# Values' two parts in one 128-column stationary block, and global queries' softmax transposed in float32 without a copy

## The chip, the cores and the metric

The kernel runs on one core of one Trainium2 chip. The time is device microseconds (us) of one execution on that core; a run's figure is a median over repeated executions. The profile is that of one execution, and its span is the time from the first to the last recorded instruction.

## The reference, cut to what matters

Attention with local and global tokens is followed by a two-layer network with a gated activation. All arrays are float32.

```python
B, H, Sl, D = 8, 8, 512, 64;  Sg = 32           # batch, heads, local and global tokens, head size
k_all = concat([k_g, k_l]); v_all = concat([v_g, v_l])
out_g = softmax(q_g @ k_all.T / 8) @ v_all      # each global query sees all 544 keys
s_ll  = where(|i - j| <= 32, q_l @ k_l.T / 8, -1e9)
out_l = softmax([q_l @ k_g.T / 8, s_ll]) @ concat([v_g, v_l])
x = concat([out_g, out_l]).transpose(0, 2, 1, 3).reshape(4352, 512)
h = x @ w_in                                    # 512 -> 2048
out = (h * sigmoid(h)) @ w_out                  # 2048 -> 512
```

## The kernel before, in words

**Tiles and blocks.** The 4352 rows of x are 34 tiles of 128 rows. They form 12 blocks (`SIZES`: two, ten times three, two tiles). For a block `n`, `first_layer(n, f)` makes one of 16 slices `f` of h (L563, 12 matmuls), ScalarE and VectorE apply the activation (L569 to L576), and `second_layer(n, f)` adds the slice into the block's output banks (L588 to L590), one slice later. Block 0 does this in float32 (L557, L586); from block 1 on every operand is split into a high and a low part in the faster float32r format (hi = rounded copy, lo = rest), and a product is three matmuls: hi times hi, hi times lo, lo times hi.

**Attention steps.** Attention for the local rows is cut into 128 steps `k`. A step takes one batch entry `b`, one chunk `c` of 128 rows (four of them, `NC`), and one of four head pairs `pr` (`NPR`); the two heads of a pair are `u` = 0 and 1. A step's parts are:

- `st_load`, `st_vload`: DMAs of queries, keys and values from HBM, issued on SyncE's queue (SP).
- `st_split`, `st_vsplit` (from step `KF` = 24 on, which is the 25th step): float32 to float32r parts. For the values these are `vhi` (ScalarE, L322) and `vlo` (VectorE, L323).
- `st_scores`: scores `s` (L345), band mask and minimum (L349), exponential (L353), normalising (L355 to L358), and from step 24 on a DMA copy to `rr`, whose tile is declared float32r (L365).
- `st_turn`: four TensorE transposes (L380; L378 in float32 for steps below 24) into a PSUM bank `t`; ScalarE and VectorE write the parts `pt_hi` and `pt_lo` of the transposed probabilities (L389, L390). Columns 128 to 159 of `pt` hold the global queries' transposed probabilities for the same keys; GpSimd (POOL) copies them from `pgt` (L400, L401).
- `st_out`: the product with the values into PSUM bank `o`. A local step has two key tiles `a`. With `u` and `a` and the three products this is twelve matmuls a step, each with 64 stationary columns (L423). 160 columns are streamed where the global queries take part, else 128 (`a` = 1 in the chunks `c` = 0 to 2). Then, for each `u`, ScalarE takes `xh` (L434) and VectorE `xl` (L435) out of the bank, and VectorE adds the 32 global columns to `acc` (L440, L442).

**Global queries.** `g_load`, `g_split`, `g_scores` (L228 to L230) and `g_soft` make, for each batch entry, the softmax of the global queries in two tiles `pgs[hh]` of 128 x 544 float32. For `b` >= `GF` = 2, `g_move` copies such a tile by two DMAs into float32r tiles `r0` and `r1` (L258, L259; `r0` shares its buffers with the output tiles of L599). `g_turn` transposes them: four 128 x 128 transposes into a bank `o` (`gt`, L276) and one of 128 x 32 into a bank `s` (`gu`, L279), and ScalarE copies both to `pgt` (L277, L280). For `b` < 2 the transposes read the float32 tile itself.

**Banks.** While block 0 is prepared there are three banks for `s`, two for `t` and three for `o`. After that there is one of each, so that each new `o`, `gt` or second `gs` waits until the last content of bank `o` has been read, and a new `s` until `gu` has been copied.

**What sets the order.** Every part of a step has a due time in steps (`DUE`, `HEAD`, `TURN`, `MOVE`); `stream` is sorted by it. `fill` deals the stream out between the matmuls of the two layers. TensorE's instructions stay in the order in which they are written; those of the other engines, and the DMA issues on SP, are put in order at build time by a scheduler with its own time estimates. Each engine runs its queue strictly in order.

Of the kernel before, what the change touches and what calls it, by code (L numbers as in the profile page):

```python
# [9 lines left out]
F32 = mybir.dt.float32  # L10
# [41 lines left out]
MOVE, TURN = (-0.3, -0.8), (0.7, 1.7)  # L52
MOVE0, TURN0 = (0.1, 0.8), (1.5, 3.6)
# [5 lines left out]
def attention_moe_kernel(ctx: ExitStack, tc: tile.TileContext, qk0_in, qk_in, v_in, gqk, wts, out):  # L59
# [154 lines left out]
    def g_scores(b, p):  # L214
        did(("scores", b, p), *([("turn" if b <= GF else "move", b - 1, p // 2)] if b else []))
# [36 lines left out]
    def g_move(b, hh):  # L252
        did(("move", b, hh), ("soft", b, hh))
        if b < GF:
            return
        r0 = two.tile([P, 4 * P], F32R, tag="o", name=f"rg0_{b}_{hh}")
        r1 = two.tile([P, SG], F32R, tag="rg", name=f"rg1_{b}_{hh}")
        nc.sync.dma_start(out=r0.bitcast(F32), in_=pgs[hh][:, : 4 * P])  # L258
        nc.sync.dma_start(out=r1.bitcast(F32), in_=pgs[hh][:, 4 * P :])  # L259
        state["rg", hh] = r0, r1  # L260

    def g_turn(b, hh):
        whole = b < GF
        if whole:
            r0, r1, idt = pgs[hh], pgs[hh][:, 4 * P :], ident.bitcast(F32)
        else:
            (r0, r1), idt = state.pop(("rg", hh)), ident
        did(("turn", b, hh), ("turn", b, 0) if hh else ("last", b - 1))
        if hh == 0:
            state["pgt"] = work.tile([P, 5, H, SG], F32, tag="pgt", name=f"pgt{b}")  # L270
        pgt = state["pgt"]
        hs = slice(4 * hh, 4 * hh + 4)
        tb = attbank("o", f"gt{b}_{hh}")
        for i in range(4):
            sl = slice(i * P, (i + 1) * P)
            nc.tensor.transpose(tb[:, sl] if whole else tb[:, sl].bitcast(F32R), r0[:, sl], idt)  # L276
        nc.scalar.copy(out=pgt[:, 0:4, hs, :], in_=tb.rearrange("p (t h q) -> p t h q", t=4, h=4))  # L277
        tb = attbank("s", f"gu{b}_{hh}")
        nc.tensor.transpose(tb[:SG, :P] if whole else tb[:SG, :P].bitcast(F32R), r1, idt)  # L279
        nc.scalar.copy(out=pgt[:SG, 4, hs, :], in_=tb[:SG, :P].rearrange("p (h q) -> p h q", h=4))  # L280
# [35 lines left out]
    def st_vsplit(k, b, c, pr):  # L316
# [3 lines left out]
        vhi = two.tile([P, 2, 2, D], F32R, tag="vhi", name=f"vhi{k}")  # L320
        vlo = two.tile([P, 2, 2, D], F32R, tag="vlo", name=f"vlo{k}")
# [3 lines left out]
        tiles["v", k] = vhi, vlo  # L325
# [42 lines left out]
    def st_turn(k, b, c, pr):  # L368
# [12 lines left out]
        t4 = t.rearrange("p (u a q) -> p u a q", u=2, a=2)  # L381
        if whole:
            pt = tiles["pt", k] = pt_whole(k)
            if c == NC - 1:
                nc.gpsimd.memset(pt[:, :, 1, P:], 0.0)
            nc.scalar.copy(out=pt[:, :, :, :P], in_=t4)
        else:
            pt_hi, pt_lo = pt_tiles(k)
            nc.scalar.copy(out=pt_hi[:, :, :, :P], in_=t4)  # L389
            nc.vector.tensor_tensor(out=pt_lo[:, :, :, :P], in0=t4, in1=pt_hi[:, :, :, :P].bitcast(F32),  # L390
                                    op=ALU.subtract)
        did(("last", b) if (c, pr) == (NC - 1, NPR - 1) else k, ("turn", b, pr // 2))
        pgt = state["pgt"]
        for a in range(2 if c == NC - 1 else 1):
            n = P if a == 0 else SG
            g = pgt[:n, c + a, 2 * pr : 2 * pr + 2, :]
            if whole:
                nc.gpsimd.tensor_copy(out=pt[:n, :, a, P:], in_=g)
                continue
            nc.gpsimd.tensor_copy(out=pt_hi[:n, :, a, P:], in_=g)  # L400
            nc.gpsimd.tensor_tensor(out=pt_lo[:n, :, a, P:], in0=g, in1=pt_hi[:n, :, a, P:].bitcast(F32),  # L401
                                    op=ALU.subtract)

    def st_out(k, b, c, pr, t):
# [6 lines left out]
        else:  # L411
            vhi, vlo = tiles.pop(("v", k))
            pt_hi, pt_lo = pt_tiles(k)
        o = attbank("o", f"o{k}")
        wide = P + SG
        for u in range(2):
            if whole:
                terms = [(vraw, pt_f, a) for a in range(2)]
            else:
                terms = [(v, pt_hi, a) for a in range(2) for v in (vhi, vlo)] + [(vhi, pt_lo, a) for a in range(2)]  # L420
            for i, (v, pt, a) in enumerate(terms):
                m = wide if a == 0 or c == NC - 1 else P
                nc.tensor.matmul(o[:D, u * wide : u * wide + m], v[:, a, u, :], pt[:, u, a, :m],  # L423
                                 start=(i == 0), stop=(i == len(terms) - 1))
        g0 = SG * (b % 4)
        for u in range(2):
            rows = slice(D * u, D * (u + 1))
            src = o[:D, u * wide : u * wide + P]
            if n == 0 and u == 0:
                nc.scalar.copy(out=xh[rows, pr, sl], in_=src)  # L430
            elif n == 0:
                nc.vector.tensor_copy(out=xh[rows, pr, sl], in_=src)
            else:
                nc.scalar.copy(out=xh[rows, pr, sl], in_=src)  # L434
                nc.vector.tensor_tensor(out=xl[rows, pr, sl], in0=src, in1=xh[rows, pr, sl].bitcast(F32),  # L435
                                        op=ALU.subtract)
            gsrc = o[:D, u * wide + P : (u + 1) * wide]
            gdst = acc[rows, pr, g0 : g0 + SG]
            if c == 0:
                nc.vector.tensor_copy(out=gdst, in_=gsrc)  # L440
            else:
                nc.vector.tensor_tensor(out=gdst, in0=gsrc, in1=gdst, op=ALU.add)  # L442
# [43 lines left out]
    for k, (t, b, c, pr) in enumerate(steps):  # L486
# [5 lines left out]
        if j == 0:  # L492
            for hh in range(2):
                put(at + (MOVE if b else MOVE0)[hh], g_move, b, hh)
# [84 lines left out]
    def second_layer(n, f, gh, gl):  # L579
# [109 lines left out]
```

## Time and profile before

| what | value |
|---|---|
| median of 3 runs | 1088.27 us (1087.07 to 1088.36) |
| the profiled execution's own time | 1086.34 us |
| its span | 1084.6 us |
| mean granted TensorE clock | 0.989 of full |
| TensorE (PE) busy | 1053.5 us, 97% |
| weight loads (PEld) busy | 934.9 us, 86% |
| VectorE (DVE) busy | 727.4 us, 67% |
| ScalarE (ACT) busy | 693.0 us, 64% |
| GpSimd (POOL) busy | 146.5 us, 14% |
| TensorE busy from 0 to 110 us | 86.3 us |
| TensorE busy from 250 to 750 us | 499.9 us |

Matmuls overlap in the records: each is shown for longer than it keeps the next one from starting. What a matmul costs is therefore read from the start of one to the start of the next, not from its duration. The records of matmuls and of weight loads are separate rows (PE and PEld).

### The profile page before, as it was taken

The numbers are of one execution on the slowest core, as the hardware profiler recorded it, in microseconds if no ns is written. First come the engines' busy times: TensorE is split into PE (matmuls) and PEld (weight loads), VectorE is DVE, ScalarE is ACT, GpSimd is POOL, SyncE is SP. The second block draws the span as 40 slices with busy tenths as digits, with TensorE's granted clock in tenths as the row PEclk, the third lists the DMA queues.
The fourth block names the chain that finished last, engine by engine and source line by source line (L and its number), as shares of the span: only waits on it lengthen the run. The fifth ranks groups of instructions, "written<-read, shape, count | busy, mean of one in ns | idle before, by whom it ended". The sixth has DMA issues, their size and how long they took to land.

```text
span 1084.6 us, 20466 instructions
## 1 busy us (share of the span) xinstructions
PE 1053.5 (97%) x6568; PEld 934.9 (86%) x6568; DVE 727.4 (67%) x2367; ACT 693.0 (64%) x1845; POOL 146.5 (14%) x360
## 2 busy tenths in 40 slices
PE   6878999999999999999999999999999999999998
PEld 4645778989999999999999999998999999999997
DVE  5974355777677777666777877786778867753322
ACT  7875456767677766656766766776677776653232
POOL 3123542111100110000110100001000111000000
PEclk8989999999999999999999999999999999999999
DMA  9961112343334333332433433443344433310000
GB/s 351 380 189 59 57 59 76 119 146 125 111 112 142 124 107 115 116 115 82 140 110 122 149 111 109 138 135 108 111 141 125 141 114 112 112 60 20 1 30 20
DMA packets 69611, 127.29 MB, mean 117 GB/s; under 512 B 9344, under 2 KB 29312, under 8 KB 69504
## 3 DMA queue, kind: packets, MB, share of 16 engines
q1 hardware_dynamic: 69504, 125.99, 36.1%
q8 instruction: 52, 0.85, 0.3%
q14 instruction: 55, 0.45, 0.1%
HBM read 86.44 MB, written 8.91 MB: 88 GB/s over the span
## 4 chain that ended last, share of the span: by engine, by line
PE 93%; ACT 3%; DVE 2%; issue 1%; DMA 1%; ACTq 0%; DVEq 0%
PE h L563 33%; PE out L588 12%; PE out L590 11%; PE out L589 11%; PE o L423 10%; PE s L345 6%; PE t L380 3%; PE h L557 2%; PE out L586 2%; PE t L378 1%; DMA raw_w<-in_wts_dram 1%; PE gs L226 1%; PE gs L228 1%; ACT w_hi L192 1%; ACT w L179 1%
## 5 line engine op out<-in xcount | busy, mean ns | idle before, releaser
L563 PE MATMUL h<-xh,w_hi 128*128 128x384 f32 (+1 forms) x704 | 236.8, 336 | 0.0
L563 PE MATMUL h<-xh,w_lo 128*128 128x384 f32 (+1 forms) x704 | 233.5, 332 | 0.0
L563 PE MATMUL h<-xl,w_hi 128*128 128x384 f32 (+1 forms) x704 | 233.1, 331 | 0.0
L569 ACT ACTIVATE t<-h 128x384 f32<-128x384 f32 (+1 forms) x192 | 90.7, 472 | 207.3 <-PE h L563 189.4
L588 PE MATMUL out<-w_hi,gh 128*128 128x512 f32 x512 | 210.6, 411 | 0.0
L590 PE MATMUL out<-w_hi,gl 128*128 128x512 f32 x512 | 201.3, 393 | 0.0
L589 PE MATMUL out<-w_lo,gh 128*128 128x512 f32 x512 | 200.3, 391 | 0.0
L571 DVE SCALAR_TENSOR_TENSOR t<-t,h 128x384 f32<-128x384 f32 (+1 forms) x176 | 95.2, 541 | 132.6 <-ACT t L569 131.9
L563 PEld LDWEIGHTS h<-xl,w_hi 128*128 128x128 f32 x704 | 132.6, 188 | 5.4 <-issue 0.5
L563 PEld LDWEIGHTS h<-xh,w_hi 128*128 128x128 f32 x704 | 132.5, 188 | 5.4 <-issue 0.7
L400 POOL CAST pt_hi<-pgt 128x64 fp32r<-128x64 f32 (+1 forms) x132 | 39.1, 308 | 724.4 <-PE o L423 706.1
L563 PEld LDWEIGHTS h<-xh,w_lo 128*128 128x128 f32 x704 | 132.3, 188 | 0.0
L576 DVE TENSOR_TENSOR gl<-t,gh 128x384 fp32r<-128x384 f32 (+1 forms) x176 | 96.8, 550 | 46.6 <-PE out L590 42.5
L349 DVE CUSTOM_DVE_ANT_0 probs<-s,mask 128x224 f32<-128x224 f32 x244 | 85.0, 384 | 62.0 <-PE s L345 61.4
L353 ACT ACTIVATE probs<-probs,st 128x224 f32<-128x224 f32 x244 | 115.7, 475 | 11.2 <-DVE st L349 10.5
L590 PEld LDWEIGHTS out<-w_hi,gl 128*128 128x128 f32 x512 | 96.1, 188 | 22.3 <-DVE gl L576 0.3
L589 PEld LDWEIGHTS out<-w_lo,gh 128*128 128x128 f32 x512 | 97.0, 189 | 10.5
L588 PEld LDWEIGHTS out<-w_hi,gh 128*128 128x128 f32 x512 | 96.4, 188 | 10.6 <-ACT gh L575 0.4
L575 ACT CAST gh<-t 128x384 fp32r<-128x384 f32 (+1 forms) x176 | 88.3, 501 | 21.8 <-DVE t L571 17.3
L434 ACT CAST xh<-o 64x128 fp32r<-64x128 f32 x240 | 61.3, 256 | 42.5 <-PE o L423 29.4
L312 ACT CAST qk<-raw 128x704 fp32r<-128x704 f32 x100 | 78.2, 782 | 15.9 <-PE s L345 15.6
L435 DVE TENSOR_TENSOR xl<-o,xh 64x128 fp32r<-64x128 f32 x240 | 67.3, 280 | 30.9 <-ACT xh L434 27.4
(117 smaller groups left out, 1937.3 us busy)
## 6 DMA issues: line engine op xcount, KB each, us to landing
raw<-in_qk_dram SPq DMA_DIRECT2D x100, 352.0 KB, 3.0
rr<-probs SPq DMA_DIRECT2D x104, 256.0 KB, 2.3
raw_w<-in_wts_dram SPq DMA_DIRECT2D x32, 512.0 KB, 6.3
vraw<-in_v_dram SPq DMA_DIRECT2D x128, 128.0 KB, 2.4
raw_g<-in_gqk_dram SPq DMA_DIRECT2D x32, 304.0 KB, 2.9
out_dram<-o SPq DMA_DIRECT2D x32, 256.0 KB, 2.3
raw<-in_qk_dram SPq DMA_DIRECT2D x28, 240.0 KB, 4.8
rg<-pg SPq DMA_DIRECT2D x12, 256.0 KB, 2.4
```

What stands on the lines that cost most here:

```text
L312: nc.scalar.copy(out=qk, in_=raw)
L349: nc.vector.tensor_tensor_reduce(out=p[:, u, :W], in0=s[:, u * W : (u + 1) * W], in1=mask_of[c], scale=-SCALE, scalar=3.0e38, op0=ALU.add, ...
L353: nc.scalar.activation(p[:, u, :W], p[:, u, :W], AF.Exp, bias=st[:, u : u + 1], scale=-1.0, accum_out=st[:, 2 + u : 3 + u])
L423: nc.tensor.matmul(o[:D, u * wide : u * wide + m], v[:, a, u, :], pt[:, u, a, :m], start=(i == 0), stop=(i == len(terms) - 1))
L563: nc.tensor.matmul(h[:, :nt], wt, x[:, c, :nt], start=(i == 0), stop=(i == 3 * NCC - 1))
L569: nc.scalar.activation(t[:, :nt], h[:, :nt], AF.Tanh, scale=0.5)
L571: nc.vector.scalar_tensor_tensor(out=out[:, :nt], in0=t[:, :nt], scalar=1.0, in1=h[:, :nt], op0=ALU.add, op1=ALU.mult)
L575: nc.scalar.copy(out=gh[:, :nt], in_=t[:, :nt])
L576: nc.vector.tensor_tensor(out=gl[:, :nt], in0=t[:, :nt], in1=gh[:, :nt].bitcast(F32), op=ALU.subtract)
L588: nc.tensor.matmul(o, gh[:, sl], wh, start=(f == 0), stop=False)
L589: nc.tensor.matmul(o, gh[:, sl], wl, start=False, stop=False)
L590: nc.tensor.matmul(o, gl[:, sl], wh, start=False, stop=(f == NF - 1))
```

## The change

It has two parts.

**Values.** `vhi` and `vlo` become one tile `vv`, in which the two 64-column parts of a head stand side by side. From step 24 on, one matmul with a stationary block of 128 columns multiplies both parts with `pt_hi`: rows 0 to 63 of bank `o` then hold hi times hi, rows 64 to 127 lo times hi. A second one with the 64 columns of the high part adds the product with `pt_lo` to rows 0 to 63. That makes eight matmuls a step. The two halves of the bank are then added: ScalarE copies rows 64 to 127 to a new tile `xs`, VectorE adds rows 0 to 63 to it, for each `u`; `xh` and `xl` are taken from `xs` for both heads at once, and the global columns go from `xs` to `acc` on POOL. The raw values of odd steps below 24 used the buffers of `vhi` and `vlo` in turn (four in all); they now use `vv` (two).

**Global queries.** `g_move` and its DMAs are gone. `g_turn` transposes the float32 tile for all `b`. The last 32 keys go to two new tiles `pgh` and `pgl` (float32r parts, laid out by head pair), by two copies on ScalarE and two subtractions on VectorE, both of which read bank `s`; POOL copies them into `pt_hi` and `pt_lo`. The loop in `second_layer` that drew the stream forward while copies were pending is gone.

```diff
     def g_turn(b, hh):
...
-            state["pgt"] = work.tile([P, 5, H, SG], F32, tag="pgt", name=f"pgt{b}")
+            state["pgt"] = (work.tile([P, NC, H, SG], F32, tag="pgt", name=f"pgt{b}"),
+                            work.tile([P, QG], F32R, tag="pgh", name=f"pgh{b}"),
+                            work.tile([P, QG], F32R, tag="pgl", name=f"pgl{b}"))
...
-            nc.tensor.transpose(tb[:, sl] if whole else tb[:, sl].bitcast(F32R), r0[:, sl], idt)
-        nc.scalar.copy(out=pgt[:, 0:4, hs, :], in_=tb.rearrange("p (t h q) -> p t h q", t=4, h=4))
+            nc.tensor.transpose(tb[:, sl], pgs[hh][:, sl], ident.bitcast(F32))
+        nc.scalar.copy(out=pgt[:, :, hs, :], in_=tb.rearrange("p (t h q) -> p t h q", t=4, h=4))
         tb = attbank("s", f"gu{b}_{hh}")
-        nc.tensor.transpose(tb[:SG, :P] if whole else tb[:SG, :P].bitcast(F32R), r1, idt)
-        nc.scalar.copy(out=pgt[:SG, 4, hs, :], in_=tb[:SG, :P].rearrange("p (h q) -> p h q", h=4))
+        nc.tensor.transpose(tb[:SG, :P], pgs[hh][:, 4 * P :], ident.bitcast(F32))
+        for i in range(2):
+            rows, src = slice(SG * (2 * hh + i), SG * (2 * hh + i + 1)), tb[:SG, QG * i : QG * (i + 1)]
+            nc.scalar.copy(out=pgh[rows, :], in_=src)
+            nc.vector.tensor_tensor(out=pgl[rows, :], in0=src, in1=pgh[rows, :].bitcast(F32), op=ALU.subtract)
...
     def st_vload(k, b, c, pr):
         if k < KF and k % 2:
-            vraw = two.tile([P, 2, 2, D], F32, tag="vhi" if k % 4 == 1 else "vlo", name=f"vraw{k}")
+            vraw = two.tile([P, 2, 2, 2, D], F32, tag="vv", name=f"vraw{k}")[:, 0]
...
     def st_out(k, b, c, pr, t):
...
-            else:
-                terms = [(v, pt_hi, a) for a in range(2) for v in (vhi, vlo)] + [(vhi, pt_lo, a) for a in range(2)]
-            for i, (v, pt, a) in enumerate(terms):
...
-                nc.tensor.matmul(o[:D, u * wide : u * wide + m], v[:, a, u, :], pt[:, u, a, :m],
-                                 start=(i == 0), stop=(i == len(terms) - 1))
+                nc.tensor.matmul(o[:, at], vv[:, a, u].rearrange("p t d -> p (t d)"), pt_hi[:, u, a, :m],
+                                 start=(a == 0), stop=(a == 1))
+                nc.tensor.matmul(o[:D, at], vv[:, a, u, 0], pt_lo[:, u, a, :m], start=False, stop=(a == 1),
+                                 skip_group_check=(a == 1))
...
+        xs = work.tile([P, wide], F32, tag="xs", name=f"xs{k}")
         for u in range(2):
+            at = slice(u * wide, (u + 1) * wide)
             rows = slice(D * u, D * (u + 1))
...
+            nc.scalar.copy(out=xs[rows, :], in_=o[D:, at])
+            nc.vector.tensor_tensor(out=xs[rows, :], in0=o[:D, at], in1=xs[rows, :], op=ALU.add)
+        nc.scalar.copy(out=xh[:, pr, sl], in_=xs[:, :P])
+        nc.vector.tensor_tensor(out=xl[:, pr, sl], in0=xs[:, :P], in1=xh[:, pr, sl].bitcast(F32), op=ALU.subtract)
+        if c == 0:
+            nc.gpsimd.tensor_copy(out=gdst, in_=xs[:, P:])
+        else:
+            nc.gpsimd.tensor_tensor(out=gdst, in0=xs[:, P:], in1=gdst, op=ALU.add)
...
-            while ("rg", 0) in state or ("rg", 1) in state:
-                advance(stream[done][0])
```

TensorE's rows at the second head of step 52 (a `c` with 128 columns for `a` = 1), before. A name's first number is the step; the size is that of the output, stationary columns by streamed columns.

```order
L423 MATMUL o52_4770<-pt_hi_1795,vhi52_4641 64x160
L423 MATMUL o52_4770<-pt_hi_1795,vlo52_4642 64x160
L423 MATMUL o52_4770<-pt_hi_1795,vhi52_4641 64x128
L423 MATMUL o52_4770<-pt_hi_1795,vlo52_4642 64x128
L423 MATMUL o52_4770<-pt_lo_1797,vhi52_4641 64x160
L423 MATMUL o52_4770<-pt_lo_1797,vhi52_4641 64x128
```

The same place after, with the two rows behind it:

```order
L420 MATMUL o52_4700<-pt_hi_1810,vv52_4575 128x160
L422 MATMUL o52_4700<-pt_lo_1812,vv52_4575 64x160
L420 MATMUL o52_4700<-pt_hi_1810,vv52_4575 128x128
L422 MATMUL o52_4700<-pt_lo_1812,vv52_4575 64x128
L596 MATMUL out3_0_3970<-w_hi10_1266,gh3_10_4611 128x512
L597 MATMUL out3_0_3970<-w_lo10_1267,gh3_10_4611 128x512
```

Four matmuls of a step are gone, and loads of 128 and of 64 columns now alternate. Apart from the `o` rows and the operand of `gt` and `gu`, TensorE's order is the same row for row.

ScalarE's queue from the first reading of bank `o` of step 52 to the next slice's activation, before:

```order
L434 CAST xh_4_3941<-o52_4770 64x128
L353 ACTIVATE probs0_114,st54_4759<-probs0_114,st54_4759 128x224
L322 CAST vhi54_4836<-vraw54_4703 128x256
L575 CAST gh3_11_4744<-t3_11_4743 128x384
L434 CAST xh_4_3941<-o52_4770 64x128
L389 CAST pt_hi_1795<-t53_4802 128x4x128
L357 ACTIVATE probs0_114<-probs0_114,st54_4759 128x224
L569 ACTIVATE t3_12_4827<-h3_12_4814 128x384
```

And after:

```order
L444 COPY xs52_4709<-o52_4700 64x160
L313 CAST vv54_4764<-vraw54_4634 128x4x64
L344 ACTIVATE probs0_114,st54_4689<-probs0_114,st54_4689 128x224
L583 CAST gh3_11_4675<-t3_11_4674 128x384
L387 CAST pt_hi_1810<-t53_4730 128x4x128
L444 COPY xs52_4709<-o52_4700 64x160
L348 ACTIVATE probs0_114<-probs0_114,st54_4689 128x224
L446 CAST xh_4_3895<-xs52_4709 128x128
L577 ACTIVATE t3_12_4755<-h3_12_4742 128x384
```

The second reading of the bank now stands behind `pt_hi` of the next step, and a third instruction, `xh`, which waits for VectorE's sum, stands ahead of the next activation.

SP's queue near its start, where the first values, queries (`raw`) and weights (`raw_w`) are fetched, before:

```order
L298 DMA vraw5_387<-in_v_dram 128x256
L288 DMA raw2_194<-in_qk0_dram 128x480
L171 DMA raw_w0_512_218<-in_wts_dram 128x1024
L288 DMA raw3_225<-in_qk0_dram 128x480
L171 DMA raw_w1_0_240<-in_wts_dram 128x1024
L298 DMA vraw7_437<-in_v_dram 128x256
L288 DMA raw8_447<-in_qk0_dram 128x480
L288 DMA raw9_468<-in_qk0_dram 128x480
L171 DMA raw_w4_0_546<-in_wts_dram 128x1024
```

And after:

```order
L279 DMA raw2_194<-in_qk0_dram 128x480
L171 DMA raw_w0_512_223<-in_wts_dram 128x1024
L279 DMA raw3_230<-in_qk0_dram 128x480
L171 DMA raw_w1_0_245<-in_wts_dram 128x1024
L279 DMA raw8_455<-in_qk0_dram 128x480
L171 DMA raw_w4_0_554<-in_wts_dram 128x1024
L279 DMA raw9_476<-in_qk0_dram 128x480
```

The values of the odd steps 5 and 7 (and later 9 to 23) no longer stand ahead of their step; they come when the step four before has given its buffer back, and what stood behind them has moved up.

More of the change, by code (lines that the diff above doesn't have):

```diff
@@ L324, in st_vsplit @@
             out=vlo, in0=vraw, in1=vhi.bitcast(F32), op=ALU.subtract)
-        tiles["v", k] = vhi, vlo
+        tiles["v", k] = vv
     def st_scores(k, b, c, pr):
@@ L381, in st_turn @@
         t4 = t.rearrange("p (u a q) -> p u a q", u=2, a=2)
+        did(("last", b) if (c, pr) == (NC - 1, NPR - 1) else k, ("turn", b, pr // 2))
+        pgt, pgh, pgl = state["pgt"]
+        g = pgt[:, c, 2 * pr : 2 * pr + 2, :]
         if whole:
             pt = tiles["pt", k] = pt_whole(k)
+            nc.scalar.copy(out=pt[:, :, :, :P], in_=t4)
+            nc.gpsimd.tensor_copy(out=pt[:, :, 0, P:], in_=g)
             if c == NC - 1:
+                rows = slice(SG * pr, SG * (pr + 1))
+                hi, lo = (part.bitcast(F32)[rows, :].rearrange("p (u q) -> p u q", u=2) for part in (pgh, pgl))
@@ L385, in st_turn @@
                 nc.gpsimd.memset(pt[:, :, 1, P:], 0.0)
[L386 to L402, printed above, removed]
+                nc.gpsimd.tensor_tensor(out=pt[:SG, :, 1, P:], in0=hi, in1=lo, op=ALU.add)
@@ L411, in st_out @@
         else:
-            vhi, vlo = tiles.pop(("v", k))
+            vv = tiles.pop(("v", k))
             pt_hi, pt_lo = pt_tiles(k)
```

81 lines of the change are left out of this document (41 added, 40 removed).

## The prediction

> **What bounds the kernel now.** I read the page first: busy shares, the slices, the chain of work that ended last.
>
> ```profile
> PE 1053.5 (97%) x6568; PEld 934.9 (86%) x6568; DVE 727.4 (67%) x2367; ACT 693.0 (64%) x1845; POOL 146.5 (14%) x360
> ...
> PE   6878999999999999999999999999999999999998
> ...
> PE 93%; ACT 3%; DVE 2%; issue 1%; DMA 1%; ACTq 0%; DVEq 0%
> ```
>
> TensorE is 93% of the chain; only the first slices show it below 9 tenths. The windows view by stage (columns: span, then busy time of PE, PEld, DVE, ACT, POOL) says where it stands still:
>
> ```profile
> 0.00:27.00 27.00, 17.30 (x66) 12.54 (x66) 15.33 (x63) 20.03 (x55) 8.85 (x27) 0.87 0.96 351
> 27.00:75.00 48.00, 37.36 (x183) 27.13 (x184) 41.44 (x126) 41.64 (x104) 8.65 (x13) 0.91 0.82 287
> 75.00:110.00 35.00, 31.62 (x120) 20.73 (x119) 17.96 (x56) 19.70 (x52) 12.11 (x19) 0.88 0.29 93
> ...
> 250.00:500.00 250.00, 249.99 (x1643) 229.90 (x1642) 182.26 (x592) 167.41 (x448) 23.90 (x76) 1.00 0.38 118
> ```
>
> Up to 110 us TensorE idles 9.7, 10.6 and 3.4 us. Later it never waits as long as inputs come in time, VectorE being 73% and ScalarE 67% busy. So from step 24 on, a matmul slot saved is time saved, and everything added on other engines is free unless it makes TensorE wait. What a slot costs is read from start to start.
>
> **Twelve matmuls become eight.** Matmul starts of a step with 128 columns at `a` = 1, then of one with 160 throughout (timeline, TensorE; start, duration):
>
> ```profile
> 514.65 0.24 PE L423 MATMUL o<-pt_hi,vhi 128*64 128x160 f32 x1
> 514.72 0.24 PE L423 MATMUL o<-pt_hi,vlo 128*64 128x160 f32 x1
> 514.79 0.22 PE L423 MATMUL o<-pt_hi,vhi 128*64 128x128 f32 x1
> 514.85 0.22 PE L423 MATMUL o<-pt_hi,vlo 128*64 128x128 f32 x1
> ...
> 515.44 0.44 PE L588 MATMUL out<-w_hi,gh 128*128 128x512 f32 x1
> 515.73 0.39 PE L589 MATMUL out<-w_lo,gh 128*128 128x512 f32 x1
> ```
>
> ```profile
> 504.85 0.23 PE L423 MATMUL o<-pt_hi,vhi 128*64 128x160 f32 x1
> ...
> 505.74 0.43 PE L588 MATMUL out<-w_hi,gh 128*128 128x512 f32 x1
> 506.00 0.39 PE L589 MATMUL out<-w_lo,gh 128*128 128x512 f32 x1
> ```
>
> A slot is 0.89 / 12 = 0.074 us for 160 columns (504.85 to 505.74) and 0.06 for 128 (514.79 to 514.85). The twelve take 515.44 - 514.65 = 0.79 us; the first 512-column matmul behind them then holds its place for 0.29 us instead of its usual 0.23. Together 0.85 us; in the other step 0.89 + 0.03 = 0.92. The 0.06 and 0.03 come from loading weights. Starts of loads (timeline, PEld), behind the twelve, and within the scores:
>
> ```profile
> 505.66 0.19 PEld L588 LDWEIGHTS out<-w_hi,gh 128*128 128x128 f32 x1
> 505.77 0.19 PEld L589 LDWEIGHTS out<-w_lo,gh 128*128 128x128 f32 x1
> ```
>
> ```profile
> 513.63 0.19 PEld L345 LDWEIGHTS s<-qk 128*128 128x128 f32 x1
> 513.74 0.19 PEld L345 LDWEIGHTS s<-klo,qk 128*128 128x128 f32 x1
> ```
>
> A 128-column load begins when the matmul before it begins, and the next follows no sooner than 0.11 us later. Under a 0.23 us matmul that is hidden; under one of 160 columns 0.11 takes the place of 0.07. Loads of 64 columns have never held the twelve back: their bound is below 0.06.
>
> In the new order (hi with a 128-column load, then lo with a 64-column load) each hi matmul keeps its own slot, 0.074 or 0.060, and covers the small load; each lo matmul covers a large load and lasts 0.11. For two `u`: 2 x (0.074 + 0.11 + 0.060 + 0.11) = 0.71 us, against 0.85; with 160 columns throughout 4 x (0.074 + 0.11) = 0.74, against 0.92. I take gains of 0.15 and 0.19. How many steps of each kind there are, the groups by form tell:
>
> ```profile
> L423 PE MATMUL o<-pt_hi,vlo 128*64 128x160 f32 x264 | 57.7, 237 | 0.0
> ...
> L423 PE MATMUL o<-pt_hi,vlo 128*64 128x128 f32 x152 | 33.8, 222 | 0.0
> ```
>
> 152 / 2 = 76 steps of the first kind, (264 - 152) / 4 = 28 of the second: 76 x 0.15 + 28 x 0.19 = **16.7 us**.
>
> The row-based price is a load of 0.11 us. The Trainium skill, TensorE: Matmul & The Clock Gate, section LDWEIGHTS (loading the stationary operand), gives columns / 1.2 ns for a load, whatever the depth; that speaks against the change, because a block twice as wide takes twice as long to load. Its 0.107 us for 128 columns would make the sum 17 us; the trace agrees with it.
>
> **Transposes in float32.** One `g_turn` now, and a float32 turn of an early step at full clock:
>
> ```profile
> 510.32 0.45 PE L276 MATMUL gt<-ident,rg 128*128 128x128 f32 x4
> 510.61 0.22 PE L279 MATMUL gu<-ident,rg 128*32 128x128 f32 x1
> 510.67 0.44 PE L588 MATMUL out<-w_hi,gh 128*128 128x512 f32 x1
> 510.95 0.40 PE L589 MATMUL out<-w_lo,gh 128*128 128x512 f32 x1
> ```
>
> ```profile
> 66.81 0.60 PE L378 MATMUL t<-ident,probs 128*128 128x128 f32 x4
> 67.25 1.02 PE L586 MATMUL out<-w,gh 128*128 128x512 f32 x2
> ```
>
> Now 0.35 us to the next matmul and 0.05 hidden in that one: 0.40. In float32 0.44 / 4 = 0.11 each, five of them 0.54. Twelve turns (b = 2 to 7, two each): 12 x 0.14 = **+1.7 us**. The 24 DMA issues that go free SP's queue and the output buffers; nothing on TensorE waits for them now. What `gt` waits for is bank `o`:
>
> ```profile
> PE gt L276 <- issue: 1.8, 1, 1.8
> ```
>
> This one wait of 1.8 us (at 753 us, until VectorE had emptied the bank) and five of under 0.2 depend on the order of the queues. Emptying took ScalarE, VectorE, VectorE for each `u` and now takes ScalarE, VectorE; but the second reading stands behind the next step's `pt_hi`. I take 0, bounds -2 and +2.
>
> **Bank `s` behind `gu`.** Before, one copy; now two copies and two subtractions, in ScalarE's order with the cast of `gh` between the copies. The turn at 864 us (ScalarE, then TensorE's next use of the bank):
>
> ```profile
> 864.60 0.61 ACT L277 COPY pgt<-gt 128x512 f32<-128x512 f32 x1
> 865.07 0.26 ACT L280 COPY pgt<-gu 32x128 f32<-32x128 f32 x1
> 865.23 0.51 ACT L575 CAST gh<-t 128x384 fp32r<-128x384 f32 x1
> ```
>
> ```profile
> 866.37 0.26 PE L345 MATMUL s<-qk 128*128 128x224 f32 x1
> ```
>
> The copies of 32 rows cost about 0.2 us each (the nearest row is 0.26 for twice the columns), `gh` 0.5, the two subtractions about 0.4 with the hand-over: the bank is free near 865.07 + 0.2 + 0.5 + 0.2 + 0.4 = 866.4, just when it is needed. Seven first turns lie like this, second turns later. I take **+1.5 us**, bounds 0 and +4 (seven times 0.5).
>
> **The longer way from `o` to x.** The work on ScalarE and VectorE, from the page:
>
> ```profile
> L434 ACT CAST xh<-o 64x128 fp32r<-64x128 f32 x240 | 61.3, 256 | 42.5 <-PE o L423 29.4
> ...
> L435 DVE TENSOR_TENSOR xl<-o,xh 64x128 fp32r<-64x128 f32 x240 | 67.3, 280 | 30.9 <-ACT xh L434 27.4
> ```
>
> ScalarE goes from two instructions of 0.26 to three of about that length, 0.3 us a step more in some 7 us; VectorE from two of 0.28 and two small ones to three of about 0.3, the same. Throughput covers that. Latency: x is whole after four alternating hand-overs and `xh`, `xl`, some 1 us later than now, and `pt_lo` is wanted by the second matmul, not the fifth. The tightest places I found, VectorE's rows and TensorE's use:
>
> ```profile
> 780.94 0.28 DVE L435 TENSOR_TENSOR xl<-o,xh 64x128 fp32r<-64x128 f32 x1 [0.28 <-ACT xh L434]
> ```
>
> ```profile
> 781.95 0.34 PE L563 MATMUL h<-xh,w_hi 128*128 128x384 f32 x1
> ```
>
> ```profile
> 820.12 0.69 DVE L390 TENSOR_TENSOR pt_lo<-t,pt_hi 128x512 fp32r<-128x512 f32 x1
> ```
>
> ```profile
> 820.90 0.23 PE L423 MATMUL o<-pt_hi,vhi 128*64 128x160 f32 x1
> ```
>
> A block start with 0.73 us to spare, and a step with 0.1. Ten block starts and a few steps like these: **+2 us**, bounds 0 and +7 (ten starts and ten steps at 0.35).
>
> **The start.** Steps below 24 keep their matmuls; the order of loads changes. A load of odd values is 128 KB:
>
> ```profile
> vraw<-in_v_dram SPq DMA_DIRECT2D x128, 128.0 KB, 2.4
> ```
>
> At the 351 GB/s of the first window 0.37 us each: weights behind them land up to 0.4, later 1 to 2 us sooner, but ScalarE's queue now has the first `pt` behind two weight conversions. TensorE idles here anyway (23.7 us), so a delay of one item can pass to the end. I take 0; bounds -4 and +5, a sixth to a fifth of that idle time, for no row prices a reordering.
>
> **Sum.** -16.7 + 1.7 + 0 + 1.5 + 2 + 0 = -11.5 us on the profiled execution, 1086.34 us by the table above (a span of 1084.6 and 1.7 around it): 1074.8. The median of the three runs, 1088.27, is 1.9 above that execution; from it the forecast is **1076.8 us**.
>
> **Rivals.**
> 1. *The wide load is hidden.* If a lo matmul kept its 0.074 or 0.060, two of each would go per step of the first kind and four of 0.074 in the second: 76 x 0.27 + 28 x 0.30 = 28.8 us, 12 more, giving 1064.7. For it: a load's record of 0.19 us is longer than 0.11, so loads do overlap in part. Against: the loads of the scores stand 0.11 apart although a 224-column slot by the same rate is 0.10. Chance 0.06.
> 2. *Waits eat half.* TensorE gains 0.15 us a step but stands for `pt_lo`, bank `o` or x at half the steps for 0.15 us: 52 x 0.15 = 8 us on top: 1084.8. For it: the spare 0.1 us above, queues in strict order. Against: 249.99 of 250 us busy, so most steps have room. 0.13.
> 3. *The start worsens* by more than its bound, one further wait of 4 us or more for a late weight: 1081 to 1086. 0.06.
> 4. *Slower.* ScalarE's `xh` waits for VectorE's sum, and the activation and `pt_hi` of the next step stand behind it. If that held `gh` or `pt_lo` up beyond their room, TensorE would wait once a step. The change loses from 11.5 / 104 = 0.11 us a step on average; at 0.25 us it costs 26 us: 1088.3 - 11.5 + 26 = 1103. For it: `pt_hi` and `xh` both moved in the queue. Against: engines a quarter to a third idle. 0.05.
>
> **How the numbers follow.** The forecast itself (1070 to 1082) has 0.70. 0.2% of 1088.27 is 2.2 us, about what a measurement of this kernel tells from no change. Faster than 1086.1: the forecast, rival 1, nearly all of 2 and 3: 0.89. Within: 0.06. Slower: rival 4 with a tail of 3, 0.05. The range goes down to the sum with the four unknown costs at their lower bounds (1.5 + 2 + 2 + 4 us less: 1067.3) and up to rival 2: 1067 to 1085, leaving out rival 1, the tail of 3, and 4.
>
> **What the changed profile would show.** The twelve turns with their transposes 0.11 us apart, and 104 x 4 = 416 matmuls fewer; starts in a step at 0.07, 0.11, 0.06, 0.11. If the lo to hi distance is 0.07, rival 1 holds. Releasers of idle time ahead of `s` after `gu`, of the first L563 of a block, and of `o` show the added waits. The windows to 110 us against those above show the start. The forecast is wrong if a load's slot is not 0.11, or if idle time of TensorE after 250 us exceeds 5 us.

## The result, and the profile after

The changed kernel takes 1080.57 us (median of 4 runs, 1080.11 to 1082.01) against 1088.24 (4 runs): a ratio of 0.9934, 95% interval 0.9917 to 0.9951, faster by 7.7 us. The forecast was 1076.8. The profiled execution took 1080.11 us, its span is 1078.3.

The page's busy times, the slices of TensorE and the chain:

```profile
PE 1044.3 (97%) x6152; PEld 926.6 (86%) x6152; DVE 746.1 (69%) x2295; ACT 731.1 (68%) x1965; POOL 185.5 (17%) x464
...
PE   5888999999999999999999999999999999999998
...
PE 91%; ACT 3%; DVE 3%; issue 2%; DMA 1%; SPq 0%; POOL 0%; ACTq 0%; POOLq 0%; DVEq 0%
```

416 matmuls are gone (6568 to 6152). TensorE is still the bound, with a little less of the chain. The windows by stage (span, then busy time of PE, PEld, DVE, ACT, POOL):

```profile
0.00:27.00 27.00, 14.43 (x50) 9.96 (x50) 15.93 (x61) 19.63 (x51) 8.88 (x26) 0.87 0.95 346
27.00:75.00 48.00, 41.66 (x206) 30.11 (x207) 41.99 (x134) 43.56 (x113) 10.10 (x17) 0.91 0.84 298
...
250.00:500.00 250.00, 249.71 (x1538) 229.83 (x1537) 187.68 (x570) 179.62 (x485) 35.69 (x107) 1.00 0.36 114
500.00:750.00 250.00, 247.40 (x1537) 227.18 (x1536) 194.62 (x599) 187.45 (x510) 38.61 (x117) 1.00 0.38 120
750.00:960.00 210.00, 209.16 (x1286) 191.86 (x1286) 160.42 (x490) 152.90 (x415) 31.06 (x92) 0.99 0.36 114
```

Two things stand out: TensorE was busy for less time up to 27 us than before (14.4 us, not 17.3) and for more from 27 to 75 (41.7, not 37.4), and it stood still for 2.6 us between 500 and 750. A step with 128 columns at `a` = 1 (timeline, TensorE, then its weight loads):

```profile
510.92 0.24 PE L420 MATMUL o<-pt_hi,vv 128*128 128x160 f32 x1
511.00 0.24 PE L422 MATMUL o<-pt_lo,vv 128*64 128x160 f32 x1
511.07 0.26 PE L420 MATMUL o<-pt_hi,vv 128*128 128x128 f32 x1
511.17 0.23 PE L422 MATMUL o<-pt_lo,vv 128*64 128x128 f32 x1
...
511.59 0.44 PE L596 MATMUL out<-w_hi,gh 128*128 128x512 f32 x1
511.87 0.39 PE L597 MATMUL out<-w_lo,gh 128*128 128x512 f32 x1
```

```profile
511.00 0.19 PEld L420 LDWEIGHTS o<-pt_hi,vv 128*128 128x128 f32 x1
511.11 0.14 PEld L422 LDWEIGHTS o<-pt_lo,vv 128*64 128x64 f32 x1
```

The eight take 511.59 - 510.92 = 0.67 us, and the `out` behind them 0.28 instead of 0.23: 0.72 together, where 0.71 was forecast. A wide load holds the next load back by 0.11 us, as it did before.

Where the time went was added up between two points that both kernels have: the start of the 25th and of the 192nd group of the first layer. (A group is the matmuls of one slice of h; ScalarE's first activation on it, L569 before and L577 after, is called its tanh below.) Each matmul counts from its start to the next one's; what exceeds its own columns' time counts as a wait. Before it is 871.21 us, after 867.40:

| item between the two points | before | after | difference |
|---|---|---|---|
| matmuls of `o` (1224, 816) | 84.28 | 69.23 | -15.05 |
| global turns, `gt` and `gu` with gaps between the `gt` | 4.67 | 5.82 | +1.15 |
| waits ahead of `gt` (bank `o`) | 2.90 | 4.50 | +1.60 |
| waits ahead of `s` behind `gu` | 0 | 1.15 | +1.15 |
| waits ahead of and within `o` | 0.40 | 1.94 | +1.54 |
| slower groups directly behind the longest wait | 0 | 1.6 | +1.6 |
| matmuls of the first layer (2004 in each) | 343.17 | 344.63 | +1.46 |
| matmuls of the second layer (1461 in each) | 345.07 | 347.86 | +2.79 |
| matmuls of `s`, `t` and `gs` | 90.7 | 90.7 | 0 |
| all | 871.21 | 867.40 | -3.8 |

The slower groups are those that ran at half the clock behind the longest wait. Of the 4.25 us that the matmuls of the two layers lost, some 0.4 belongs to the turns: the matmul directly behind a `gu`, mostly an `out`, now holds its place longer (0.32 us for an `out`, before 0.28).

Ahead of these points the kernel gained 2.5 us more (204.07 to 201.61 us), which makes the span's 6.3. The waits view of TensorE from 205 us on names four kinds:

```profile
PE gt L264 <- DVE xs L445: 3.5, 6, 2.0
PE s L336 <- DVE pgl L271: 1.0, 1, 1.0
PE o L420 <- DVE xs L445: 0.6, 1, 0.6
PE o L422 <- DVE pt_lo L388: 0.4, 1, 0.4
```

The longest of them, on TensorE and then VectorE:

```profile
745.37 0.40 PE L598 MATMUL out<-w_hi,gl 128*128 128x512 f32 x1
747.78 0.63 PE L264 MATMUL gt<-ident,pg 128*128 128x128 f32 x4 [2.01 <-DVE xs L445]
```

```profile
744.80 0.32 DVE L445 TENSOR_TENSOR xs<-o,xs 64x160 f32<-64x160 f32 x1
...
745.87 0.56 DVE L584 TENSOR_TENSOR gl<-t,gh 128x384 fp32r<-128x384 f32 x1
...
746.59 0.69 DVE L388 TENSOR_TENSOR pt_lo<-t,pt_hi 128x512 fp32r<-128x512 f32 x1
747.31 0.32 DVE L445 TENSOR_TENSOR xs<-o,xs 64x160 f32<-64x160 f32 x1
```

Between the two sums that empty bank `o` stand `gl` and the next step's `pt_lo`; the second sum ends at 747.63 and `gt` starts. This is the wait of 1.8 us that the kernel before had at 753 us, a little longer.

Two items were in no step of the forecast: the same matmuls of both layers became slower, and behind the long wait the clock fell (both below).

### The profile page after: what moved, and what is told of

Same layout as the page of the kernel before. It is cut to its first block, busy times and chain, and to the rows that moved or that the text cites. A ratio compares the mean times of both kernels' runs of the same rounds, so it can differ in the third digit from the quotient of the medians.

```text
span 1078.3 us, 19847 instructions
## 1 busy us (share of the span) xinstructions
PE 1044.3 (97%) x6152; PEld 926.6 (86%) x6152; DVE 746.1 (69%) x2295; ACT 731.1 (68%) x1965; POOL 185.5 (17%) x464
## 4 chain that ended last, share of the span: by engine, by line
PE 91%; ACT 3%; DVE 3%; issue 2%; DMA 1%; SPq 0%; POOL 0%; ACTq 0%; POOLq 0%; DVEq 0%
PE h L571 33%; PE out L596 11%; PE out L598 11%; PE out L597 11%; PE s L336 6%; PE o L420 4%; PE o L422 3%; PE t L371 3%; PE out L594 3%; PE o L416 2%; PE h L565 2%; PE t L369 1%; PE gt L264 1%; DMA raw_w<-in_wts_dram 1%; PE gs L228 1%
## 5 line engine op out<-in xcount | busy, mean ns | idle before, releaser
L577 ACT ACTIVATE t<-h 128x384 f32<-128x384 f32 (+1 forms) x192 | 90.6, 472 | 160.8 <-PE h L571 147.8
L579 DVE SCALAR_TENSOR_TENSOR t<-t,h 128x384 f32<-128x384 f32 (+1 forms) x176 | 95.2, 541 | 115.4 <-ACT t L577 114.5
L584 DVE TENSOR_TENSOR gl<-t,gh 128x384 fp32r<-128x384 f32 (+1 forms) x176 | 97.3, 553 | 40.0 <-PE out L598 34.7
L390 POOL CAST pt_hi<-pgt 128x64 fp32r<-128x64 f32 x104 | 35.2, 339 | 481.1 <-PE o L422 305.2
L597 PEld LDWEIGHTS out<-w_lo,gh 128*128 128x128 f32 x512 | 96.9, 189 | 10.9
L445 DVE TENSOR_TENSOR xs<-o,xs 64x160 f32<-64x160 f32 x208 | 65.5, 315 | 23.5 <-ACT xs L444 19.3
L420 PE MATMUL o<-pt_hi,vv 128*128 128x160 f32 (+1 forms) x416 | 80.9, 263 | 0.7 <-DVE xs L445 0.6
```

What stands on the lines that cost most here:

```text
L420: nc.tensor.matmul(o[:, at], vv[:, a, u].rearrange("p t d -> p (t d)"), pt_hi[:, u, a, :m], start=(a == 0), stop=(a == 1))
L577: nc.scalar.activation(t[:, :nt], h[:, :nt], AF.Tanh, scale=0.5)
L579: nc.vector.scalar_tensor_tensor(out=out[:, :nt], in0=t[:, :nt], scalar=1.0, in1=h[:, :nt], op0=ALU.add, op1=ALU.mult)
L584: nc.vector.tensor_tensor(out=gl[:, :nt], in0=t[:, :nt], in1=gh[:, :nt].bitcast(F32), op=ALU.subtract)
L597: nc.tensor.matmul(o, gh[:, sl], wl, start=False, stop=False)
```

## The experiments

Ratios are to the kernel before on the same chip, with their 95% interval.

**Both kernels once more.**

> The kernel before, unchanged, profiled once more. The first two profiles differ in something the change does not touch: between 160 and 960 us the same 512-column matmuls of the second layer stand 228 ns apart before and 232 ns after, the 384-column ones 174.6 and 175.8, together 4.3 us. Theory program: the gap belongs to the two programs, so this profile shows 228 to 229 ns again. Rival execution: it belongs to the single execution, and this profile may show 232 as well, or anything between 228 and 233. Time 1087 to 1088.5 either way.

> The changed kernel, unchanged, profiled once more. Theory program: 232 ns for the second layer's matmuls again, TensorE waits again about 2.0 us for bank o at 745 us, and the granted clock falls to a half for some 3 us directly after it. Rival execution: the spacing comes out near 228 ns, or the wait or the fall of the clock is absent, and 1.5 us of the loss was chance. Time 1080 to 1082 either way.

Times 1089.6 (above the 1088.5 that was expected) and 1080.96 us. Between the same two points the first layer takes 343.02 and 344.63 us, the second 345.11 and 347.89: the slower matmuls belong to the program. The wait at 745 us and the slow groups behind it came back in the changed kernel. But the kernel before, with none in its first profile, now had such slow groups too (1.5 us), so they aren't the change's alone.

**The two parts apart.** In `values_only`, the changed kernel, `g_turn` again has

```diff
-            nc.tensor.transpose(tb[:, sl], pgs[hh][:, sl], ident.bitcast(F32))
+            nc.tensor.transpose(tb[:, sl] if whole else tb[:, sl].bitcast(F32R), r0[:, sl], idt)
```

with `g_move` and its two DMAs (one small statistics tile has one buffer instead of two, for room). `queries_only` is the kernel before with the changed `g_turn` and POOL copies.

> The changed kernel with the global queries' transposes put back as they were: DMA copies to a float32r tile and float32r transposes (the copies of the last 32 keys stay as changed). It isolates the eight matmuls. Theory: the float32 transposes cost 0.09 us a turn, 12 turns 1.1 us, and the DMA copies were free, so 1079.5 against 1080.6 for the whole change; TensorE's wait for bank o near 745 us is still there. Rival: the slower spacing of the unchanged matmuls (4.3 us) comes from the queries' part, then about 1075 here and 228 ns in the second layer. Second rival: the copies on DMA cost something of their own, then 1081 or more.

> The kernel before with the queries' part alone: float32 transposes from the softmax's tile, no DMA copies, the last 32 keys split by ScalarE and VectorE; twelve matmuls in each step as before. Theory: 1.1 us more for the transposes and about 1 us more of waits for bank s, so 1090 against 1088.2 (ratio 1.002), with 228 ns in the second layer. Rival spacing: the slower unchanged matmuls belong to this part: 1094. Second rival: the start's gain of 2.4 us before 205 us belongs to this part: 1087.5.

`values_only`: 1077.45 us, 0.9912 (0.9897 to 0.9926). Between the points it takes 866.31 us, 1.1 less than the whole change: the price of the float32 transposes was as expected, and the copies on DMA cost nothing there. Its profile has the rest of its 3.1 us ahead of the points (the 25th group's tanh at 201.4 us, not 203.9). `queries_only`: 1088.61 us, 1.0008 (0.9997 to 1.0019): 874.15 us between the points, 2.9 more than before (turns 1.1, bank `s` 1.16, bank `o` 0.25, the rest matmuls of the second layer). Its first layer takes 343.23 us and its second 345.32, the fast values, while `values_only` has 344.55 and 347.69. So what slows the unchanged matmuls comes with the values' part. And the queries' part gained nothing: alone it is level with the kernel before, and the values' part without it (0.9912) is at least as fast as the whole change (0.9934).

**Half the stationary columns.** Edit: the hi matmul takes `vv[:, a, u, 0]` (64 columns) and writes `o[:D]`; ScalarE copies `o[:D]`. The kernel leaves out the product of the values' low part with `pt_hi`.

> The changed kernel with the hi matmul's stationary block cut to 64 columns: the product of the values' lo part with the probabilities' hi part is left out, and ScalarE's first copy reads the lower half of the bank instead, so every other instruction stays. Theory: the lo matmul's slot of 0.11 us is the next load of 128 columns; with 64 columns the eight slots are 0.074 and 0.060 again, 0.54 us instead of 0.71 in 76 steps and 0.59 instead of 0.74 in 28, together 17 us less: about 1063.5. Rival: the 0.11 us belongs to the pair of matmuls that accumulate in one bank (hi, then lo on its lower half), not to the load: then 1080.6, starts still 0.07 and 0.11 apart.

1068.15 us, 0.9818 (0.9805 to 0.9832). Timeline:

```profile
505.90 0.24 PE L420 MATMUL o<-pt_hi,vv 128*64 128x160 f32 x1
505.98 0.24 PE L422 MATMUL o<-pt_lo,vv 128*64 128x160 f32 x1
506.05 0.22 PE L420 MATMUL o<-pt_hi,vv 128*64 128x128 f32 x1
506.11 0.22 PE L422 MATMUL o<-pt_lo,vv 128*64 128x128 f32 x1
...
506.44 0.45 PE L596 MATMUL out<-w_hi,gh 128*128 128x512 f32 x1
```

Starts 0.07, 0.07, 0.06 apart, eight in 0.54 us: the rival falls, the 0.11 us is the wide load. Matmuls of `o` take 56.30 us, 12.9 less than with wide loads. My 17 counted one load too many: the `out` behind the step has a wide load of its own in either kernel. Four matmuls fewer would give 28.0 us; the wide loads take 12.9 of them back. Not all of the 12.9 reached the end: between the points it takes 856.50 us, 10.9 less than after. TensorE came to bank `o` sooner and waited there some 4 us longer, while the slow groups (1.6) were absent:

```profile
PE gt L264 <- DVE xs L445: 7.3, 6, 1.9
```

**Where the tiles lie.** The diff has one more effect that is easily overlooked. Ahead of the pool that holds the values, `x`, `t`, `gh` and `gl`, the new tile `xs` adds 640 bytes a partition, and `pgt`, `pgh` and `pgl` together take 512 fewer than `pgt` did. So these tiles lie 128 bytes further on: by the addresses in the compiled program at 64 modulo 512 bytes of a partition, where they were at 448. Edit of `after_shifted` (of `queries_shifted` the first two lines alone, with 32 columns):

```diff
+    gap = two.tile([P, 48], F32, tag="gap", bufs=1, name="gap")
+    nc.gpsimd.memset(gap, 0.0)
...
+    small = ctx.enter_context(tc.tile_pool(name="small", bufs=4))
     two = ctx.enter_context(tc.tile_pool(name="two", bufs=2))
-    small = ctx.enter_context(tc.tile_pool(name="small", bufs=4))
```

> The changed kernel with 384 bytes a partition put ahead of one pool (192 of a dummy tile, 192 of the pool of small statistics, which moves there), so that the tiles of x, gh and gl start at the same place modulo 512 bytes as in the kernel before (448 instead of 64). No instruction of the work changes. Theory layout: the unchanged matmuls of both layers are 0.5% slower only for these addresses, so the second layer's slot falls from 232 to 228 ns, the first's from 175 to 174, and the time by 4 us to 1076.5. Rival: what slows them is the changed work beside them (ScalarE, VectorE and GpSimd are busier); then 232 ns and 1080.6 stay.

> The mirror of it: the kernel with the queries' part alone (1088.6, 228 ns), its tiles of x, gh and gl shifted by a dummy tile of 128 bytes to 64 modulo 512 bytes, as in the changed kernel. Theory layout: 232 and 175 ns and 4 us more, 1092.5. Rival: 228 ns and 1088.6 stay.

`after_shifted`: 1074.54 us, 0.9877 (0.986 to 0.9893), 2 us better than expected. `queries_shifted`: 1092.91 us, 1.0045 (1.0029 to 1.006). Both go the way that the layout theory said, by its size or more. Two more, both of `queries_only`: the gap ahead of `t`, `gh`, `gl` alone, and a gap of 256 bytes ahead of all:

> The kernel with the queries' part alone, with a dummy tile of 128 bytes between the tiles of x and those of t, gh, gl: only these three move, from 448 to 64 modulo 512 bytes; x stays at 448. Theory stationary: what is slow is a matmul whose stationary block (gh, gl) lies at 64, so the second layer's slot goes to 232 ns and the first layer's (stationary weights, moving x) stays at 174. Rival moving: the first layer's depends on x and the second's on neither, then both stay at 174 and 228. Time within 0.3% of 1088.6 either way.

> The kernel with the queries' part alone, with x, t, gh and gl all shifted by 256 bytes, from 448 to 192 modulo 512. Theory period 256: what counts is the place modulo 256 bytes (192 in the fast kernels, 64 in the slow ones), so 174 and 228 ns stay and the time is 1088.6. Rival period 512 or more: 192 is another place than 448, and the slots may come out at 175 and 232 or at anything else, with the time up to 4 us longer.

1094.66 and 1090.24 us, one execution each. The first lies outside the 0.3% around 1088.6 that was expected: besides the slower second layer it had 1.7 us of slow groups, and its start was 2.6 us later than that of `queries_only`. Groups of TensorE's instructions from 250 to 960 us (times, busy us, mean ns of one); in this order before, after, `after_shifted`, then `queries_shifted`, `gh_shifted`:

```profile
L563 PE MATMUL h<-xh,w_lo 128*128 128x384 f32 x512 | 172.3, 336 | 0.0
...
L589 PE MATMUL out<-w_lo,gh 128*128 128x512 f32 x384 | 150.0, 391 | 0.0
```

```profile
L571 PE MATMUL h<-xh,w_lo 128*128 128x384 f32 x519 | 175.9, 339 | 0.0
...
L597 PE MATMUL out<-w_lo,gh 128*128 128x512 f32 x387 | 152.3, 394 | 0.0
```

```profile
L599 PE MATMUL out<-w_lo,gh 128*128 128x512 f32 x390 | 152.2, 390 | 0.0
```

```profile
L584 PE MATMUL out<-w_lo,gh 128*128 128x512 f32 x381 | 150.0, 394 | 0.0
```

```profile
L556 PE MATMUL h<-xh,w_lo 128*128 128x384 f32 x508 | 170.9, 336 | 0.0
...
L585 PE MATMUL out<-w_lo,gh 128*128 128x512 f32 x381 | 150.1, 394 | 0.0
```

A `w_lo` matmul of the second layer with its stationary `gh` at 64 is recorded 3 to 4 ns longer and holds its place for 232 ns instead of 228 (medians of some 385 each, from start to start); those of `w_hi` with `gl` hold it for 2 ns longer, those of `w_hi` with `gh` for no longer that is clear. `gl` moves with `gh` in every run, so the two aren't told apart. In `gh_shifted`, where `x` stays at 448, the first layer keeps its 336 ns. From start to start its matmuls of `xl` with `w_hi` take 174.6 ns in the mean before, 175.8 after, and 174.4, 175.6 and 174.3 in the other three in the order above. With all of them at 192, in `queries_shifted_256`, both layers take what they took without it (343.17 and 345.31 us between the points). So the place in a partition decides, for the moving `x` and for the stationary `gh` and `gl` alike: 3.9 us less in `after_shifted` and 4.0 more in `queries_shifted` between the points. Only 64 (slow), 192 and 448 (both fast) modulo 512 were tried. That 192 is as good as 448 fits the theory that only the place modulo 256 counts, but a second slow place, 320, was not tried; why they differ stays open.

**The turns later.**

```diff
-TURN = (0.7, 1.7)
+TURN = (0.9, 1.9)
...
-        tb = attbank("s", f"gu{b}_{hh}")
+        tb = attbank("t", f"gu{b}_{hh}")
```

> The changed kernel with the global queries' turns due 0.2 steps later (0.9 and 1.9 instead of 0.7 and 1.7) and the 32-row transpose in bank t instead of bank s. At all twelve turns at least 1.6 us of matmuls now stand between o and gt (0.9 at seven of them before). Theory: the waits for bank o (five of 0.46 us, one of 2.2), for bank s (1.15 us) and the half clock after the long wait (some 1.5 us) go: 5 to 6 us less, 1075; the idle time of TensorE after 250 us falls from 6 us to under 3. Rival: the waits only move, to o behind gt or to t behind the 32-row transpose, and the time stays at 1080 to 1081.

1081.83 us, 0.9944 (0.9932 to 0.9956): no gain in all. TensorE's waits from 205 us on:

```profile
PE o L422 <- DVE pt_lo L388: 1.2, 4, 0.5
...
PE gu L267 <- DVE pt_lo L388: 0.4, 2, 0.2
PE o L420 <- ACT pt_hi L387: 0.4, 1, 0.4
```

The waits of `gt` and `s` are gone (5.65 us), and so are the slow groups; waits of `o` for `pt_hi` and `pt_lo`, of `gu` for bank `t` and at a few places around `out` took back some 4. Between the points 864.49 us remain, 2.9 less than after. They were lost earlier: the 25th group's tanh came at 208.6 us instead of 203.9. `TURN` also places the second batch's turns, but these stand at 117 and 125 us in the changed kernel; ahead of them TensorE's order is the same row for row, and yet the seventh group's tanh was 6.5 us late (101.8 against 95.2). The longest of the added waits there, up to 205 us, in `turn_later` and then after:

```profile
PE gs L226 <- DVE acc L438: 5.9, 2, 4.8
```

```profile
PE gs L226 <- DVE acc L438: 1.8, 1, 1.8
```

What the edit changes that early is the bank of the first batch's `gu`. No run has that alone, so what cost the start is not shown. Neither theory held: the waits moved in part, and the loss was at the start.

**Both finds together.** `after_shifted`, with the new times from the third batch on, and `gu` in bank `t` except where bank `s` has room (three turns, and the first two batches):

```diff
+TURN0, TURN1 = (1.5, 3.6), (0.9, 1.9)
...
-                put(at + (TURN if b else TURN0)[hh], g_turn, b, hh)
+                put(at + (TURN0 if b == 0 else TURN if b < GF else TURN1)[hh], g_turn, b, hh)
```

> Both finds together, as a candidate that beats both kernels: the shifted layout of after_shifted, and the turns due at 0.9 and 1.9 from the third batch on only (the second batch keeps its old place, since turn_later lost about 4 us before 205 us), the 32-row transpose in bank t except at three turns where bank t had been read too late and bank s is not wanted for 2 us. Theory: from 205 us on, the 3.0 us that turn_later gained and the 3.9 us of the layout add up, and 1 us of waits for bank t goes too: 1070.5 (after_shifted 1074.5, the changed kernel 1080.6). Rival: the gain of turn_later was only the half clock after the long wait (1.3 us): then 1073.

1069.98 us (1068.36 to 1072.46), 0.9839 (0.9824 to 0.9855): the gains add up, and this version beats both kernels. It leaves the first two batches' turns and banks as they were, and its 25th group's tanh comes at 200.6 us.

**The start.** The odd values' loads two to a tile:

```diff
+            if k % 4 == 1:
+                state["odd"] = two.tile([P, 2, 2, 2, D], F32, tag="vv", name=f"vraw{k}")
+            vraw = state["odd"][:, k % 4 // 2]
```

> The changed kernel with the odd values of the first 24 steps loaded two to a tile of the new shape, so that four of them have a place again (as before the change) instead of two. The two loads that the change moved from places 16 and 21 of SP's queue to 37 and later stand at 16 and 21 again. Across the profiles so far the seventh group of the first layer begins at 98.1 us in the mean of six of programs with the old values part (95.4 to 100.0) and at 94.2 in six with the new one (92.2 to 96.1). Theory places: the start's gain of 3.6 to 3.9 us comes from the weights going ahead of these loads, so here it is lost: that group begins near 98 us and the time is 1084. Rival: the gain comes from elsewhere (the order of ScalarE's and VectorE's first instructions), or is only the spread of single executions; then 94 to 96 us and 1080.6.

1079.28 us, 0.992 (0.9905 to 0.9934): not slower, so the theory of the loads' places falls as a cause of the median's gain. In the one profile the start was as late as before the change (seventh group's tanh at 97.3 us, 25th at 206.0), but one execution can't tell: of four programs that differ from `queries_only` by a dummy tile at most, the seventh group's tanh came at 95.4 to 99.4 us.

## Why the prediction was right, and where it was off

The sign, the range and the main mechanism held; the gain was 7.7 us, not 11.5. That the miss is not larger is in part luck: the start gave 2.5 us in the profiled execution that no term had forecast.

- *Twelve matmuls become eight*, forecast -16.7: -15.05. The mechanism is shown by `narrow_hi`: a load of 128 columns behind a short matmul costs its 0.11 us, and rival 1 is out (its sum, 76 x 0.27 + 28 x 0.30, is 28.9, not 28.8). By the Trainium skill's rule (TensorE: Matmul & The Clock Gate, section LDWEIGHTS), columns / 1.2 ns, such a load is estimated at 0.107 us; the trace agrees, with 0.109 us between the starts at 511.00 and 511.11. 0.6 us of the shortfall goes with the layout: in `after_shifted`, where the values move too, the eights take 68.62 us in all.
- *Float32 transposes*, +1.7: +1.15 in their own places, and some 0.4 in the matmul behind, so nearly as forecast. The four stand 0.11 us apart; `gu` keeps only 0.03 us, but the `out` behind it then holds its place for 0.32:

```profile
506.44 0.60 PE L264 MATMUL gt<-ident,pg 128*128 128x128 f32 x4
506.88 0.27 PE L267 MATMUL gu<-ident,pg 128*32 128x128 f32 x1
506.90 0.47 PE L596 MATMUL out<-w_hi,gh 128*128 128x512 f32 x1
507.22 0.39 PE L597 MATMUL out<-w_lo,gh 128*128 128x512 f32 x1
```

- *Bank `o` ahead of `gt`*, 0 with bounds of 2: +1.6. The text saw that the second reading stands behind `pt_hi`, and still took 0; the sums on VectorE also stand behind `gl` and `pt_lo`. And it left out what can follow such a wait, the slow groups, another 1.6 in this execution; whether they come is chance, as the two profiles of the kernel before show.
- *Bank `s` behind `gu`*, +1.5: +1.15, at one turn only (241 us), not at seven.
- *The longer way to x*, +2: +1.54, all of it ahead of or within `o`; no block's first matmul had to wait.
- *The start*, 0 with bounds of -4 and +5: -2.5 in this execution. The seventh group's tanh came at 95.4 to 100.0 us in the six profiles of programs with the old values' part (mean 98.1) and at 92.2 to 96.1 in six with the new (mean 94.2); the other two with the new had it at 101.8 (`turn_later`) and 97.3 (`four_buffers`). Up to 110 us the recorded clock stood at a half for 19.4 us in the mean of the former six and 14.8 of the latter, which may have a share in this. How much of the median's gain lies there, and why, is open.
- *Not in the sum*: the place of `x`, `gh` and `gl` in a partition, 3.9 of the 4.25 us that the two layers lost. That matmuls which the diff doesn't touch keep their slot was taken for granted. This is the step that failed: at the old places (`after_shifted`) the change gives 1074.5, 2.3 under the forecast.
- Rival 2 had waits as the loss, but twice its size and not its kind: waits at half the steps didn't come; waits at a few turns did. Rivals 3 and 4 didn't occur.
- The forecast's own test, idle time of TensorE after 250 us above 5 us, wasn't met: 0.3, 2.6 and 0.8 us up to 960, and none from there to 1068.

## What to carry to other kernels

Before giving a wide stationary block credit for the matmuls that it saves, charge each of its loads against the matmul ahead of it: here 28.0 us of slots saved cost 12.9. When a change adds or drops tiles, compare the start-to-start times of matmuls that it doesn't touch, by form, first: half a per cent over both layers was worth half of the net gain here, and 384 bytes put ahead of them gave it back. A transpose that needs a bank belongs where every reader of that bank has long been served in its queue's order. And the start of a kernel is to be compared for itself: `turn_later` lost there what it gained later on.

## What the runs showed of the hardware that was not expected

**The place in a partition.** The float32r matmuls of this kernel with moving or stationary operands at 64 modulo 512 bytes of a partition were slower from start to start than at 192 or 448: the first layer by 0.4% (175 against 174 ns for 384 columns in the median), the second by 0.7% (232 against 228 ns for `w_lo` with `gh`, little or nothing for `w_hi` with `gh`).

**Half the clock after a wait of about 2 us.** Windows of the changed kernel around the long wait (the third number from the right is the granted clock):

```profile
745.40:747.80 2.40, 0.39 (x3) 0.05 (x1) 2.02 (x7) 1.48 (x4) 0.09 (x1) 1.00 0.68 205
747.80:749.00 1.20, 1.20 (x9) 1.19 (x10) 0.29 (x1) 0.72 (x2) 0.16 (x1) 0.96 0.58 219
749.00:752.00 3.00, 3.00 (x12) 3.00 (x11) 0.43 (x2) 0.43 (x3) 0.00 (x0) 0.50 0.00 0
```

The clock fell 1.1 us after work had begun again and stayed at a half for 3.4 us; first-layer matmuls then stood 0.32 us apart instead of 0.175, 1.5 to 1.7 us in all in the executions that show it. Twelve profiled executions have such a wait, with TensorE idle for 1.76 to 2.01 us; six show the fall, the kernel before in one of two.

The traces tell what sets them apart. In all fourteen, every fall and rise of the granted clock but the last rise stands a whole number of 3.413 us behind the first fall, as on a grid. In all six with a fall the wait lay whole between two neighbouring points of this grid, and the clock fell at the second, 0.2 to 1.5 us after work had begun again; here the points are 745.50 and 748.91, the wait 745.77 to 747.78. In five of the six without it a point of the grid lay within the wait: in the kernel before at 752.56, the wait from 752.20 to 753.96. The sixth, `queries_only`, is an exception: its wait lay whole between two points, and the clock didn't fall. How much of a stretch must be idle is not shown, as 1.76 us were enough in `again_before` and 1.86 were not in `four_buffers`. Where the grid lies against the wait differs between executions of one kernel, so whether the 1.6 us are lost is luck.

The Trainium skill (TensorE: Matmul & The Clock Gate, Part 1: The HAM clock gate) tells of a free-running window of 3413 ns and of a drop after an idle one. The grid and the length at half clock agree with it; but the windows behind which the clock fell here were idle, by the records, for only 1.76 to 2.01 us.
